# Block-decay attention and an MLP on one core: fewer unread matmuls, an earlier AV, one copy on another engine, one split step

## The chip, the cores and the metric

The kernel runs on one core of a Trainium2 chip. A core has TensorE (PE, matmuls; its weight loads are listed as PEld), VectorE (DVE), ScalarE (ACT), GpSimd (POOL) and SyncE (SP, which only issues DMAs here). Each engine works through its own instructions in program order, and engines wait for each other by semaphores. The metric is the time of one execution on the device in microseconds; lower is better.

## The reference, cut to what matters

An attention with a decay per head, computed over blocks, feeds a layer norm, a two-matrix MLP and a residual. Inputs are float32.

```python
# q, k, v: (4, 8, 768, 64); lam: one decay per head; block = 64
for b in range(nb):
    intra = einsum('bhic,bhjc->bhij', qb, kb) * Dmask      # lam^(i-j) for i >= j
    intra = einsum('bhij,bhjd->bhid', intra, vb)
    inter = einsum('bhid,bhde->bhie', qb * lam_pow, kv_state)
    out[b] = intra + inter
    kv_state = lam**64 * kv_state + einsum('bhsd,bhse->bhde', kb * rev_pow, vb)
x  = heads joined: (4, 768, 512)
xn = (x - mean) / sqrt(var + 1e-6) * g_ln
y  = x + relu(xn @ w_ch1) @ w_ch2                          # 512 -> 2048 -> 512
```

## The kernel before, in words

**Tiling.** The 768 rows of each of the 4 batches are cut into 3 windows of 256 rows. That makes 12 units of work `u` (the change's "pairs": pairs of 128-row tiles `ab` = 0, 1); units 0 to 3 are the first windows of the four batches. The MLP works on groups `g` of two tiles, one group per unit, so that group 0 is the first and group 2 the third.

**The attention of a unit.** `open_window` makes its bf16 buffers; `in_k_one`, `in_q_one`, `in_v` scale and cast the loaded k, q and v into them. `transpose_pe(u, a, pairs, eng)` (L253, L254) transposes k (`a` = 0) or q (`a` = 1) by matmuls against an identity into a PSUM tile `tp`, and one copy brings it to `kqT`: on VectorE if `eng` is given, else on ScalarE. `scores` (L282) multiplies k^T with q^T into PSUM tiles `sc` (`sce` when early), `mask` (L292, VectorE) brings them masked to `mA`. `kv` (L316) forms the products of k and v, `new_state` turns them into the running state. `av` (L428) multiplies the masked scores with v into `po`, and `inter` (L441) adds the product of q with the state, in two parts, `inter(u, 0)` and `inter(u, 1)`; between them `reader` (L452) has VectorE read a column of `po`. `norm` (L474, L475, L479 for the first two units) takes mean and variance on VectorE and writes the centred and scaled `xc`; `to_xT(u, ab)` transposes it by four matmuls (L502) and a ScalarE copy (L503) into `xT`.

**The MLP of a group.** The first matrix W1 lies in four pieces `w1[0..3]` of 512 columns, the second, W2, in four pieces as well, each loaded by one DMA that POOL issues (L117, L120). A step `m1(u)` (L539) is 8 matmuls of 256 columns over both tiles of the group, and one ReLU on ScalarE (L542) of 128x512; two steps use one piece of W1. `m1s(f, c, lo, hi)` issues the steps on piece `c`: `m1s(m1a, 2, 0, 1)` is the first of the two, `m1s(m1a, 2, 1, 2)` the second. `m1.tile(c, i)` (L650, ReLU L653) does the piece `c` for tile `i` alone: 16 matmuls of 128 columns. `m2` (L676) multiplies with W2, four matmuls of 512 columns per step; from group 4 on another form (L574) with fewer multiplications takes its place, which uses sums formed ahead on VectorE. PSUM tiles of both share the tag `mm` with four buffers, in rotation, together with `tp`, `xt` and `sce`.

**What sets the order.** The kernel is written with a manual schedule: the order of calls is the order on each engine. The head (the first 37 us) is written out by hand: units 0 and 1 with the MLP of groups 0 (`m1a`) and 1 (`m1b`) between them. After that a list `plan` holds the MLP's steps, and `units(n)` takes the next n of them between the attention steps of later units. The plan's first 20 steps are groups 0 and 1; then come the steps of group 2. Unit 2 begins with `transpose_pe(2, 0, ...)` for k^T, one step, and `transpose_pe(2, 1, ...)` for q^T.

**The start.** While the first k and q are being loaded, TensorE runs small matmuls of the identity into a tile `unread` (L180), which nothing reads, and then a matmul that spreads g_ln over the partitions (`g_all`, L183).

Of the kernel before, what the change touches and what calls it, by code (L numbers as in the profile page):

```python
# [17 lines left out]
def kernel(  # L18
# [11 lines left out]
    nc = tc.nc  # L30
# [31 lines left out]
    def mm_tile(shape, dtype, name):  # L62
        return ps.tile(shape, dtype, tag="mm", bufs=4, name=name)
# [111 lines left out]
    nc.vector.memset(ones, 1.0)  # L175
    nc.vector.tensor_copy(keep64[half[1]], keep64_b[half[1]])
    unread = ps.tile([128, 32], F32, tag="po0", name="unread")
    for _ in range(26):
        for b in range(2):
            nc.tensor.matmul(unread[half[b]], lhsT=ident[half[0], half[b]], rhs=ident[half[0], 0:32],  # L180
                             start=True, stop=True, skip_group_check=True)
# [19 lines left out]
    def open_window(u):  # L201
        kq = wk.tile([128, 2, NP, 2, 2, D], BF16, tag="kq", bufs=3, name="kq")
        vb = wk.tile([128, H, 2, D], BF16, tag="vb", bufs=4, name="vb")
        st[u] = dict(kq=kq, vb=vb)
        if u < XB:
            st[u]["kqT"] = wk.tile([128, 2, NP, 2, 128], BF16, tag="kqT", bufs=3, name="kqT")
# [40 lines left out]
    def transpose_pe(u, a, pairs, eng=None):  # L247
        s = st[u]
        n = len(pairs)
        tp = mm_tile([128, n, 2, 128], BF16, "tp")  # L250
        for i, p in enumerate(pairs):
            for j in range(2):
                nc.tensor.transpose(tp[:, i, j, :], s["kq"][:, a, p, j], ident)  # L253
        (eng.tensor_copy if eng else nc.scalar.copy)(s["kqT"][:, a, pairs[0]:pairs[0] + n], tp)  # L254
# [69 lines left out]
    def state_sum(u, ab):  # L324
        tmp = wk.tile([128, NP, D], F32, tag="Stmp", name="Stmp")
        nc.vector.tensor_tensor(tmp, st[u]["pk"][ab], state[u % B], op=ALU.add)  # L326
        return tmp
# [91 lines left out]
    def av(u, pairs, chunks=(0, 1)):  # L419
        s = st[u]  # L420
        if "po" not in s:
            s["po"] = [ps.tile([128, H, D], F32, tag=f"po{ab}", name=f"po{ab}") for ab in range(2)]
        for p in pairs:
            for e in range(2):
                for j in range(2):
                    for jq in range(2):
                        for ab in chunks:
                            nc.tensor.matmul(s["po"][ab][half[jq], 2 * p + e, :],  # L428
                                             lhsT=s[f"mA{p // 2}"][half[ab], e, p % 2, j, half[jq]],
                                             rhs=s["vb"][half[ab], 2 * p + e, j],  # L430
                                             start=(p == 0 and e == 0 and j == 0), stop=False, skip_group_check=True)

    def inter(u, first, fence=True):


        s = st[u]
        qT = s["kqT"][:, 1]
        todo = [(e, p, ab, jq) for p in range(NP) for jq in range(2)
                for e, ab in ((first, 0), (1 - first, 1)) if s["S"][ab][jq] is not None]
        for i, (e, p, ab, jq) in enumerate(todo):  # L440
            nc.tensor.matmul(s["po"][ab][half[jq], 2 * p + e, :], lhsT=qT[half[e], p, jq, half[ab]],  # L441
                             rhs=s["S"][ab][jq][half[e], p, :],
                             start=False, stop=(first == 1 and i >= len(todo) - 4), skip_group_check=True)
        if first == 0 and fence:
            reader(u)
# [8 lines left out]
    def norm(u, ab, early=False):  # L454
        s = st[u]
        po = s["po"][ab].rearrange("p h d -> p (h d)")
        if "x" not in s:
            s["x"] = xp.tile([128, 2, DM], F32, tag="x", bufs=6, name="x")
            s["mv"] = xp.tile([128, 2, 2], F32, tag="mv", name="mv")
            s["xc"] = wk.tile([128, 2, DM], BF16, tag="xc", name="xc")  # L460
        x, mv, xc = s["x"][:, ab], s["mv"][:, ab], s["xc"][:, ab]
        if u >= 2:
            if ab == 0:
                s["sum"] = xp.tile([128, 2], F32, tag="sum", name="sum")
                s["nmean"] = xp.tile([128, 2], F32, tag="nmean", name="nmean")
            sm, nm = s["sum"][:, ab:ab + 1], s["nmean"][:, ab:ab + 1]
            nc.scalar.activation(x, po, ACT.Copy, accum_out=sm)  # L467
            nc.scalar.activation(nm, sm, ACT.Copy, scale=-1.0 / DM)  # L468
            nc.vector.scalar_tensor_tensor(xc, in0=po, scalar=nm, in1=g_row, op0=ALU.add, op1=ALU.mult)  # L469
            return  # L470
        if not early:
            nc.scalar.copy(x, po)
        stats = wk.tile([128, 6], F32, tag="stats", name="stats")
        nc.vector.bn_stats(stats, po if early else x)  # L474
        nc.vector.bn_aggr(mv, stats)  # L475
        n_h = 2 if u == 0 else 1
        for h in range(n_h):
            sl = slice(h * DM // n_h, (h + 1) * DM // n_h)
            nc.vector.scalar_tensor_tensor(xc[:, sl], in0=po[:, sl], scalar=mv[:, 0:1], in1=g_row[:, sl],  # L479
                                           op0=ALU.subtract, op1=ALU.mult)  # L480
# [5 lines left out]
    def to_xT(u, ab):  # L486
        s = st[u]
        t = 2 * u + ab
        g = group_of[t]
        i = t - groups[g][0]  # L490
        if i == 0:
            xT_of[g] = gp.tile([128, KA, GT * 128], BF16, tag="xT", bufs=3, name="xT")
        dst = xT_of[g][:, :, i * 128:(i + 1) * 128]
        if u >= 2 and u not in X_PE:
            nc.sync.dma_start_transpose(dst, s["xc"][:, ab])
        else:
            if u < 2:
                xt = mm_tile([128, KA, 128], BF16, "xt")
            else:
                xt = ps.tile([128, KA, 128], BF16, tag=f"po{ab}", name="xt")  # L500
            for kk in range(KA):
                nc.tensor.transpose(xt[:, kk, :], s["xc"][:, ab, kk * 128:(kk + 1) * 128], ident)  # L502
            nc.scalar.copy(dst, xt)  # L503
# [280 lines left out]
    m1a, m2a = mlp(0)  # L784
    m1b, m2b = mlp(1)

    def m1s(f, c, lo=0, hi=2):
        n = f.count // NWC
        for u in range(c * n + lo * n // 2, c * n + hi * n // 2):
            f(u)  # L790
# [208 lines left out]
    kv(1, "sc")  # L999
    new_state(1, 0, nc.scalar)  # L1000
    m1s(m1a, 1, 1, 2)
    m1s(m1a, 2, 0, 1)
    av(1, (0, 1))
    av(1, (2, 3))
    inter(1, 0)
    norm(1, 0, early=True)
    m1s(m1a, 2, 1, 2)
    inter(1, 1)
    norm(1, 1, early=True)
    st[1]["tmp"] = state_sum(1, 1)  # L1010
    m1s(m1a, 3, 0, 1)
    to_xT(1, 0)
    m1s(m1a, 3, 1, 2)
    m1b.tile(0, 0)
    to_xT(1, 1)
    m1b.tile(1, 0)
    open_window(2)
    in_k_one(2, nc.vector, 0)
# [16 lines left out]
    plan = [(m1b.tile, c, i) for c in (2, 3) for i in range(2)]  # L1035
    plan += [(m2, i, part) for part in range(KB // 4) for m2, i in ((m2a, 0), (m2a, 1), (m2b, 0))]
    plan += [(m2b, 1, part) for part in range(KB // 4)]
    for g in range(2, len(groups)):
        m1, m2 = mlp(g)
        plan += [(m1, n) for n in range(m1.count)]  # L1040
        if g >= WG:
            plan += [(m2.w, n) for n in range(8)]
        else:
            plan += [(m2, i, part) for i in range(len(groups[g])) for part in range(KB // 4)]
# [3 lines left out]
    def units(n):  # L1048
        for _ in range(n):
            f, *a = next(steps)  # L1050
            f(*a)


    transpose_pe(2, 0, (0, 1, 2, 3))
    units(1)
    transpose_pe(2, 1, (0, 1, 2, 3))
    new_state(0, 1, nc.gpsimd)
# [314 lines left out]
```

## Time and profile before

| what | value |
|---|---|
| time, median of 3 runs | 208.91 us (208.74 to 209.30) |
| time of the profiled execution | 208.85 us |
| its span, first to last instruction | 207.1 us |
| busy in the span: PE, PEld | 198.3, 159.4 us |
| busy in the span: DVE, ACT, POOL | 133.6, 121.5, 84.7 us |
| TensorE instructions: matmuls, weight loads | 3199, 3199 |
| HBM read, written | 27.27, 6.29 MB |

The profile is that of one execution. A line of the timeline has the start, the duration, the engine, the line of the kernel, the operation with output<-inputs, the form, and in brackets the idle time of the engine before it with what ended it. In the row of slices each digit is the busy share of a fortieth of the span in tenths. In the chain of waits each row has a start, a duration and the work that the end of the kernel hung on at that time; "issue" is time without a wait that the profile shows. TensorE's matmuls overlap, so the spacing of their starts tells more than their durations.

### The profile page before, as it was taken

Reading aid. Unit: us, or ns where it says so; the run is one execution under the profiler, and the core shown is the slowest. Engines: PE = TensorE matmul, PEld = TensorE weight load, DVE = VectorE, ACT = ScalarE, POOL = GpSimd, SP = SyncE. Lnnn points to the kernel's source line nnn. Section 1 sums busy time; section 2 is a strip of 40 time slices with the busy share of each in tenths; the row PEclk is TensorE's granted clock in tenths of the full one; section 3 lists DMA queues with packets and bytes.
Section 4 is the critical chain, followed back from the end, with each engine's and each line's share of the span. In section 5 each row is a group of like instructions: output and inputs, shape, how many; then the busy total and the mean of one; then the engine's idle time right before and its main releaser. Section 6 shows DMA issues by size and latency. Waiting matters only on the chain.

```text
span 207.1 us, 7435 instructions
## 1 busy us (share of the span) xinstructions
PE 198.3 (96%) x3199; PEld 159.4 (77%) x3199; DVE 133.6 (65%) x276; ACT 121.5 (59%) x279; POOL 84.7 (41%) x117
## 2 busy tenths in 40 slices
PE   4989999999999999999999999999999999999992
PEld 3468889544685687488888888888888888988881
DVE  3686480526964459867898775776876947865253
ACT  3775668726258358257565775585596565652620
POOL 5658059027747260266264440782282202002020
PEclk9999999999999999999999999999999999999999
DMA  4999999999899999999999999897958020158403
GB/s 105 302 256 216 165 293 188 213 279 258 231 211 278 218 168 171 183 256 171 196 202 128 188 202 170 205 213 163 190 109 181 3 51 3 24 117 278 143 14 92
DMA packets 91011, 36.41 MB, mean 176 GB/s; under 512 B 65121, under 2 KB 88161, under 8 KB 90978
## 3 DMA queue, kind: packets, MB, share of 16 engines
q1 hardware_dynamic: 86368, 31.53, 73.5%
q0 software_dynamic: 4224, 4.19, 12.5%
q8 instruction: 25, 0.41, 0.8%
q10 hardware_dynamic: 386, 0.20, 0.4%
q14 instruction: 8, 0.07, 0.1%
HBM read 27.27 MB, written 6.29 MB: 162 GB/s over the span
## 4 chain that ended last, share of the span: by engine, by line
PE 86%; ACT 6%; DVE 2%; DMA 2%; issue 1%; POOLq 0%; POOL 0%; DVEq 0%
PE pm L539 37%; PE pm L676 14%; PE pwd L574 6%; PE pwa L574 6%; PE pwc L574 6%; PE pm1t L650 3%; PE pwb L574 3%; PE po L441 2%; DMA lam_b<-in_lam_dram 2%; PE tp L253 2%; PE po L428 2%; ACT kqT L254 1%; DVE x L587 1%; PE po L415 1%; PE xt L502 1%
## 5 line engine op out<-in xcount | busy, mean ns | idle before, releaser
L539 PE MATMUL pm<-xT,w 128*128 128x256 bf16 x688 | 78.5, 273 | 0.0
L539 PEld LDWEIGHTS <-w 128*128 128x128 bf16 x688 | 66.0, 98 | 8.8 <-DVE Smid L397 0.3
L542 ACT ACTIVATE hT<-pm 128x512 f16<-128x512 f32 x86 | 50.4, 596 | 30.9 <-PE pm L539 30.8
L676 PE MATMUL pm<-w,hT 128*128 128x512 f16 x128 | 29.8, 380 | 0.0
L574 PEld LDWEIGHTS <-hs 128*128 128x128 f16 x256 | 24.9, 98 | 2.9
L599 POOL TENSOR_TENSOR x<-ev_u,x 128x256 f32<-128x256 f32 x8 | 5.8, 724 | 51.8 <-ACT ev_u L598 40.4
L322 POOL TENSOR_TENSOR Sn<-Stmp,lam_s 128x256 bf16<-128x256 f32 x16 | 9.8, 616 | 36.8 <-DVE Stmp L326 15.7
L557 DVE TENSOR_TENSOR hs<-hT 128x1024 f16<-128x1024 f16 x16 | 13.8, 864 | 16.5 <-ACT hT L542 16.5
L676 PEld LDWEIGHTS <-hT 128*128 128x128 f16 x128 | 11.7, 98 | 12.5
L574 PEld LDWEIGHTS <-hT 128*128 128x128 f16 x192 | 18.8, 98 | 2.2
L469 DVE SCALAR_TENSOR_TENSOR xc<-po,nmean,g_row 128x512 bf16<-128x512 f32 x18 | 13.0, 745 | 5.1 <-ACT nmean L468 5.0
L467 ACT ACTIVATE x<-po 128x512 f32<-128x512 f32 x18 | 10.6, 591 | 7.7 <-PE po L441 4.5
L292 DVE TENSOR_TENSOR mA<-sc,keep 128x512 bf16<-128x512 f32 x14 | 9.0, 684 | 8.8 <-PE sc L282 8.8
L512 ACT ACTIVATE sq<-x,nmean 128x512 bf16<-128x512 f32 x18 | 12.9, 719 | 0.3
L245 POOL TENSOR_TENSOR vb<-vin,lam_v 128x1024 bf16<-128x1024 f32 (+1 forms) x7 | 11.6, 1658 | 3.4 <-DMA vin<-in_v_dram 3.2
L245 POOL TENSOR_TENSOR vb<-vin,lam_p 128x1024 bf16<-128x1024 f32 x6 | 11.6, 1928 | 0.8 <-DMA vin<-in_v_dram 0.8
L650 PE MATMUL pm1t<-xT,w 128*128 128x128 bf16 x160 | 11.2, 229 | 0.1
L650 PEld LDWEIGHTS <-w 128*128 128x128 bf16 x160 | 10.1, 103 | 0.7 <-issue 0.6
L587 DVE SCALAR_TENSOR_TENSOR x<-pwd,rstd,x 128x256 f32<-128x256 f32 x16 | 7.7, 482 | 3.6 <-POOL x L607 3.6
L239 POOL TENSOR_TENSOR kq<-qin,lam_p 128x512 bf16<-128x512 f32 x9 | 9.3, 1042 | 1.6 <-DMA qin<-in_q_dram 1.6
L587 DVE SCALAR_TENSOR_TENSOR x<-pwa,rstd,x 128x512 f32<-128x512 f32 (+1 forms) x16 | 9.1, 612 | 0.8
L574 PE MATMUL pwa<-w,hT 128*128 128x256 f16 x64 | 9.6, 273 | 0.0
(134 smaller groups left out, 315.5 us busy)
## 6 DMA issues: line engine op xcount, KB each, us to landing
out_dram<-x SPq DMA_DIRECT2D x22, 256.0 KB, 4.0
w<-in_moe_w_ch_dram POOLq DMA_DIRECT2D x8, 512.0 KB, 8.6
kin<-in_k_dram SPq DMA_DIRECT2D x14, 256.0 KB, 5.5
qin<-in_q_dram SPq DMA_DIRECT2D x14, 256.0 KB, 4.9
vin<-in_v_dram SPq DMA_DIRECT2D x14, 256.0 KB, 4.8
kin<-in_k_dram SPq DMA_DIRECT2D x5, 512.0 KB, 6.3
qin<-in_q_dram SPq DMA_DIRECT2D x5, 512.0 KB, 7.6
vin<-in_v_dram SPq DMA_DIRECT2D x5, 512.0 KB, 6.5
```

The costliest lines, as they stand in the source:

```text
L245: eng.tensor_tensor(st[u]["vb"][:, hs], qkv_in[u]["v"][:, hs], lv.to_broadcast([128, n, 2, D]), op=ALU.mult)
L322: eng.tensor_tensor(dst, src, lam_s[:, :, None].to_broadcast([128, NP, D]), op=ALU.mult)
L467: nc.scalar.activation(x, po, ACT.Copy, accum_out=sm)
L469: nc.vector.scalar_tensor_tensor(xc, in0=po, scalar=nm, in1=g_row, op0=ALU.add, op1=ALU.mult)
L512: nc.scalar.activation(sq, s["x"][:, ab], ACT.Square, bias=s["nmean"][:, ab:ab + 1], accum_out=ss[:, ab:ab + 1])
L539: nc.tensor.matmul(pm[:, b, :], lhsT=w1[n // W2K][:, kk, (n % W2K) * 128:(n % W2K + 1) * 128], rhs=xT_of[g][:, kk, 0:N], start=(b == 0 and ...
L542: nc.scalar.activation(hT[:, u * NB:(u + 1) * NB, 0:N], pm, ACT.Relu)
L557: nc.vector.tensor_tensor(s13, b[:, :, 1:2, :].to_broadcast([128, n, 2, 128]), b[:, :, 0:4:3, :], op=ALU.subtract)
L574: nc.tensor.matmul(pr[bank], lhsT=lhs(r), rhs=rhs, start=(first and r == 0), stop=(r == KB // 2 - 1), skip_group_check=True)
L587: nc.vector.scalar_tensor_tensor(out, in0=in0, scalar=r[ab], in1=in1, op0=ALU.mult, op1=ALU.add)
L650: nc.tensor.matmul(pm[:, b, :], lhsT=w1[c][:, kk, b * 128:(b + 1) * 128], rhs=xT_of[g][:, kk, i * 128:(i + 1) * 128], start=(b == 0 and kk ...
L676: nc.tensor.matmul(acc[i], lhsT=hT[:, kk, i * 128:(i + 1) * 128], rhs=w2[kk // W2K][:, kk % W2K, :], start=(kk == 0), stop=(kk == KB - 1))
```

## The change

Four edits. The unread matmuls go from 52 to 36, which with their weight loads are 32 instructions. In the hand-written head, the second unit's `av`, `inter` and `norm` go ahead of the first step on W1's third piece, and the steps of pieces 3 and 4, the transposes of the second unit's `xc` and the tiles of group 1 are interleaved anew. The third unit's k^T is copied out of PSUM by VectorE instead of ScalarE. And the first two steps of the third group, 8 matmuls over both tiles each, become two `m1.tile` steps of 16 matmuls over one tile each, on the same piece of W1.

```diff
     unread = ps.tile([128, 32], F32, tag="po0", name="unread")
-    for _ in range(26):
+    for _ in range(18):
         for b in range(2):
             nc.tensor.matmul(unread[half[b]], lhsT=ident[half[0], half[b]], rhs=ident[half[0], 0:32],
                              start=True, stop=True, skip_group_check=True)
...
     kv(1, "sc")
     new_state(1, 0, nc.scalar)
     m1s(m1a, 1, 1, 2)
-    m1s(m1a, 2, 0, 1)
     av(1, (0, 1))
     av(1, (2, 3))
     inter(1, 0)
     norm(1, 0, early=True)
-    m1s(m1a, 2, 1, 2)
+    m1s(m1a, 2, 0, 1)
     inter(1, 1)
     norm(1, 1, early=True)
     st[1]["tmp"] = state_sum(1, 1)
+    m1s(m1a, 2, 1, 2)
+    to_xT(1, 0)
     m1s(m1a, 3, 0, 1)
-    to_xT(1, 0)
-    m1s(m1a, 3, 1, 2)
     m1b.tile(0, 0)
     to_xT(1, 1)
+    m1s(m1a, 3, 1, 2)
     m1b.tile(1, 0)
...
-        plan += [(m1, n) for n in range(m1.count)]
+        plan += [(m1.tile, 0, 0), (m1.tile, 0, 1)] if g == 2 else [(m1, 0), (m1, 1)]
+        plan += [(m1, n) for n in range(2, m1.count)]
...
-    transpose_pe(2, 0, (0, 1, 2, 3))
+    transpose_pe(2, 0, (0, 1, 2, 3), nc.vector)
     units(1)
     transpose_pe(2, 1, (0, 1, 2, 3))
```

## The prediction, made before the result was known

> **What bounds the kernel now.** I read the page first: busy shares, then the row of slices.
>
> ```profile
> PE 198.3 (96%) x3199; PEld 159.4 (77%) x3199; DVE 133.6 (65%) x276; ACT 121.5 (59%) x279; POOL 84.7 (41%) x117
> ...
> PE   4989999999999999999999999999999999999992
> ```
>
> TensorE has work from the second slice to the last. Busy is not peak, so I took the spacing of matmul starts in the trace: after 37 us it is the ordinary one almost everywhere (216 ns at 512 columns, 109 to 111 ns at 256, 56 ns at 128). A change of order there gains nothing; only holes in TensorE's stream do. I looked for them in the chain of waits (start us, us, what), between 26 and 38 us:
>
> ```profile
> 27.60 0.60 ACT hT L542
> 28.20 0.48 ACT xT L503
> 28.68 0.04 issue
> 28.72 1.07 PE pm1t L650 x16
> 29.79 0.02 issue
> 29.82 0.60 ACT hT L653
> 30.41 0.48 ACT xT L503
> 30.90 0.04 issue
> 30.94 1.96 PE pm1t L650 x32
> ...
> 33.52 0.97 ACT x L484 x2
> 34.48 0.92 ACT kqT L254
> 35.40 0.50 ACT hT L653
> 35.90 0.91 ACT kqT L254
> 36.82 0.04 issue
> 36.86 0.42 PE sc L282 x16
> ```
>
> Three times TensorE stands behind ScalarE. In starts: the matmul at 28.72 comes 337 ns after the one before, where 110 is ordinary (0.23 us lost); that at 30.94 after 262 instead of 56 (0.21 lost); the scores at 36.86 after 573. Ordinary there is 149: a change from a full to a small tile costs 93 ns beside the matmul itself (202 ns start to start after 256 columns, 309 after 512), and 56 + 93 = 149; so 0.42 us is lost. The third is two k/q copies, 1.06 us each, behind two copies of x.
>
> Then TensorE's timeline ahead of the first W1 tile:
>
> ```profile
> 15.05 0.31 PE L441 MATMUL po<-Sn,kqT 64*64 64x64 bf16 x4
> 16.04 0.32 PE L441 MATMUL po<-Sn,kqT 64*64 64x64 bf16 x4 [0.67 <-issue]
> 16.29 0.61 PE L253 MATMUL tp<-ident,kq 128*128 128x128 bf16 x4
> 16.69 1.91 PE L650 MATMUL pm1t<-xT,w 128*128 128x128 bf16 x16
> ```
>
> Eight matmuls of one loop are cut in two, with no semaphore between the halves: start to start 0.91 us. Last, the list of waits of TensorE for the head:
>
> ```profile
> PE g_all L183 <- DVE keep L176: 1.2, 1, 1.2
> ```
>
> The matmul behind the unread ones waits 1.2 us for VectorE anyway.
>
> **What the Trainium skill says.** "Runtime: NRT & Kernel Launch", Instruction fetch mechanics: engines refill instructions in blocks of 16 KiB, 256 instructions, and a crossing is mostly hidden. The page has 25 instruction packets of together 0.41 MB on queue 8, so 16 KB each, and 6398 TensorE instructions: it fits. The first of them starts at 13.66 us, and the cut above follows it, at about the 449th TensorE instruction; so here a crossing is seen. At later packets no hole appears. "TensorE: Matmul & The Clock Gate", Part 1: The HAM clock gate: cold TensorE runs at half speed until a busy window of a free-running 3.41 us has passed. The trace agrees: 128-column matmuls start every 107 ns until 19.1 us and every 56 ns from 20.4 us; its clock record begins full speed at 20.5 us. "VectorE: DVE Perf Modes", Why PSUM operands drop a tier: a 16-bit copy out of PSUM can still go at twice the rate. The four kqT copies by VectorE take 418 ns for 128x512, against ScalarE's 586: it agrees.
>
> **The change, part by part.**
>
> *Sixteen unread matmuls with their weight loads go.* Fifty-two start between 1.43 and 2.79 us, 27 ns apart: 16 x 27 = 0.43 us of TensorE time, worth nothing, since g_all starts at 4.18 behind VectorE's copy (ends 4.07). If that cover went, 0.43 us. But every later instruction stands 32 places earlier, so the fetch boundary falls 32 named instructions later: behind the other four matmuls of the state product and four transposes, at about the eighth matmul of the first W1 tile. TensorE reached this at 17.4 us; the block was there at 16.04. The fetch will start a little later, since the sequencer has 32 more instructions to issue; I expect it still in time, and no hole. What is late next: the first W1 piece. Its DMA issued at 8.07 took 8.5 us, landing at 16.58, and the tile started at 16.69. So of 0.88 us pause, 0.05 us is gained; bounds: 0 to 0.11 us. VectorE's normalisation (statistics at 16.39, idle 1.01 us before) comes up to 0.9 us earlier, but TensorE gets to its transposes only at 18.82, paced by itself: nothing.
>
> *AV of the second pair ahead of W1's third piece.* No instruction is added. TensorE's order becomes: half of piece 2, AV, half of piece 3, second state product, half of piece 3, transposes, half of piece 4, tile (0,0) of group 1, transposes, the last half of piece 4, tile (1,0). AV starts at 24.52 - 0.87 = 23.65; its masks are done at 22.56 and the state from ScalarE at 23.82, while the state product comes only at 24.18. VectorE's reader, statistics and centring follow 0.87 earlier: xc(1,0) at 26.30, transposes at 26.53 (before: 27.17 and 27.40). The stretch up to tile (0,0) is the old one shifted by one step of 0.87 us, so its 0.23 us hole stays: still activation, xT copy, tile on ScalarE. The step that was displaced now stands behind the second transposes: ScalarE gets 0.88 us more for the second xT, so the hole at 30.94 closes: -0.21 us. W1 pieces: third landed at 23.49, needed now at 24.42 (before 23.54, on its heels); fourth landed at 26.05, needed at 26.75 and 28.96. The moved steps issue no DMA and nothing on POOL, so SP's and POOL's queues keep their order. VectorE's later casts move from 29.03 to about 28.15; k has landed by 27.89, q's wait at 30.14 remains, and its user is TensorE at 34 us.
>
> *k^T of the third pair copied by VectorE.* ScalarE loses 1.06 us between 34.36 and 35.40; VectorE gains one 128x1024 copy, not shown there: between 0.42 x 2 = 0.84 and, at ScalarE's rate, 1.06 us; I take 0.84. VectorE is idle for 6.49 us before its masks at 37.31; behind the copy only those wait. It runs from about 33.2 to 34.0. ScalarE, worked forward: x until 34.3, one activation until 34.8, q^T until 35.75. TensorE, 0.21 us ahead, has finished its two tiles at about 36.1, so the scores no longer wait: -0.42 us. If ScalarE is late after all, I get back between 0 and 0.42.
>
> *Two tiles in the third group.* Two steps of 8 matmuls at 109 ns (0.874 us each; 54.33 to 57.82 for four) become two of 16 at 56 ns (0.891 us each, from 28.72 to 29.61): +0.035 us, bounds 0 to 0.1. ScalarE evicts 512 columns each in either form; its inputs were ready at 51.2, the steps begin at 54.3. These add 32 instructions, so from there fetch boundaries stand as before.
>
> Sum: -0.05 - 0.21 - 0.42 + 0.04 = **-0.64 us**. TensorE takes that to the end: W2's last piece landed at 45.93 and is needed after 48; kqT of pairs 3 and 4 landed at 54.16 and 63.47, used at 58.2 and 70.3. Against the profiled execution's own 208.85 us (span 207.1 and 1.75 around it) this gives 208.21; the median shown is 0.06 higher, which is scatter. I say **208.2**.
>
> **Rivals.**
> 1. *The fetch hole moves into the first W1 tile.* It decides if the block lands after about 17.4 us. For it: in the old trace the queue ran dry with only some 30 instructions in hand at the packet's start. Against: without the cut TensorE stands some 0.6 us ahead of W1's landing, time in which the block can come. Price: up to 0.88 us on the path, and by thinning the window before 20.5 us it may put full speed off by one window, half of 3.41 = 1.71 us. 208.2 + 0.88 = 209.1; with the clock, 210.8.
> 2. *The gain is eaten.* q^T at 35.75 against scores at 36.1 has 0.35 us in hand; if VectorE's copy stands behind a POOL operation at 33.28 (1.92 us), or the clock phase slips, the holes close only in part: 208.6 to 208.9.
> 3. *The clock comes one window earlier*, since the pause before the dense tiles is gone. For it: work up to 20.4 is at half speed. The second W1 piece lands at 20.65 and was used at 21.33: at most 0.68 us more, 207.5.
> 4. *It does not do what it says* (the boundary is elsewhere): the first term is 0, the rest stays: 208.3.
>
> **How the numbers follow.** My forecast with case 4 has 0.61, rival 1 0.11, rival 2 0.16, rival 3 0.12. A measurement here tells about 0.3% from no change, so below 208.28 is faster and above 209.54 slower. The forecast stands close to the edge: 0.46 of its 0.61 faster, 0.15 same; rival 3 faster; rival 2 0.13 same and 0.03 slower by some new wait; rival 1 slower. Faster 0.58, same 0.28, slower 0.14. Range 207.4 (rival 3, with the best ends) to 209.2 (rival 1 without the clock).
>
> **What would show it.** Right: no cut in the state product near 15 us; first W1 tile at 16.6 to 16.7; AV at 23.65; a hole of 0.2 us ahead of tile (0,0) but none ahead of (0,1); VectorE's kqT copy of 0.7 to 0.9 us near 33; scores of the third pair within 0.15 us of the tile before. Wrong: a pause inside the first W1 tile, full clock later than 20.5 us, or scores still released by ScalarE's copy.

## The result, and the profile after

In 22 executions of each kernel the changed one has a median of 209.18 us (208.23 to 211.07) and the one before 209.34 us (208.31 to 211.51). The ratio is **0.9995, 95% interval 0.997 to 1.0019**: no difference that this comparison can tell, where 208.2 us and a gain of 0.3% were forecast. The level was missed too: the three executions shown ahead of the prediction (208.74 to 209.30, median 208.91) all lie below the median of the 22, whose spread is 3.2 us.

The profiled execution of the changed kernel took 210.09 us, with a span of 208.3 us, 1.2 us more than the one of before. First the same rows of the page:

```profile
PE 198.5 (95%) x3199; PEld 159.1 (76%) x3199; DVE 135.6 (65%) x277; ACT 120.7 (58%) x278; POOL 84.9 (41%) x117
...
PE   3989999999999999999999999999999999999991
```

VectorE has one instruction more and ScalarE one fewer; TensorE has as many as before. Next, TensorE's timeline ahead of the first W1 tile:

```profile
15.62 0.42 PE L441 MATMUL po<-Sn,kqT 64*64 64x64 bf16 x8
15.99 0.29 PE L253 MATMUL tp<-ident,kq 128*128 128x128 bf16 x1
16.57 0.50 PE L253 MATMUL tp<-ident,kq 128*128 128x128 bf16 x3 [0.29 <-POOL kq L229]
16.87 1.92 PE L650 MATMUL pm1t<-xT,w 128*128 128x128 bf16 x16
```

The state product is whole now (x8 in one row), and the tile still starts just behind the landing of W1's first piece, 16.81 us in this execution. Then the two stretches where ScalarE held TensorE up, from the same timeline, and VectorE's copies of kqT (count, duration in ns min/median/max):

```profile
28.40 1.05 PE L650 MATMUL pm1t<-xT,w 128*128 128x128 bf16 x16
29.29 0.39 PE L502 MATMUL xt<-ident,xc 128*128 128x128 bf16 x4
29.51 1.04 PE L539 MATMUL pm<-xT,w 128*128 128x256 bf16 x8
30.39 1.28 PE L650 MATMUL pm1t<-xT,w 128*128 128x128 bf16 x20
...
34.85 1.95 PE L650 MATMUL pm1t<-xT,w 128*128 128x128 bf16 x32
36.73 0.42 PE L282 MATMUL sc<-kqT 64*64 64x128 bf16 x16
```

```profile
L254 DVE COPY kqT<-tp x5: 414/419/690, 9.2 to 33.7; 128x512 bf16<-128x512 bf16 x4, 128x1024 bf16<-128x1024 bf16 x1
```

The hole of 0.21 us ahead of tile (0,1) is gone; the one of 0.42 us ahead of the third pair's scores is gone (149 ns from the last tile matmul, the ordinary step), with a VectorE copy of 0.69 us. So the two gains that made up the forecast are in the profile. What took its place? The chain of waits of this execution near 48 us, and TensorE's timeline there:

```profile
33.85 14.79 DMA w<-in_moe_w_ch_dram
48.63 0.04 issue
48.67 1.02 PE pm L676 x4
```

```profile
47.92 0.39 PE L502 MATMUL xt<-ident,xc 128*128 128x128 bf16 x4
48.67 1.02 PE L676 MATMUL pm<-w,hT 128*128 128x512 f16 x4 [0.37 <-DMA w<-in_moe_w_ch_dram]
```

W2's last piece landed at 48.63, 2.7 us later than in the profile of before, and TensorE waited. In starts of matmuls, the measure of the holes above, 0.53 us are lost there and 0.18 at W2's third piece (landing 44.94): together 0.71 us, more than the whole forecast. Already the first small DMA, the decays, issued at 0.81 us in both, landed 0.46 us later (5.02 against 4.56), and W1's first load was issued 0.46 us later (8.53 against 8.07): part of the lateness was there before the change could act.

### The profile page after: what moved, and what is told of

Its sections match the earlier page's. It is cut to its first block, busy times and chain, and to the rows that moved or that the text cites. A ratio compares the mean times of both kernels' runs of the same rounds, so it can differ in the third digit from the quotient of the medians.

```text
span 208.3 us, 7435 instructions
## 1 busy us (share of the span) xinstructions
PE 198.5 (95%) x3199; PEld 159.1 (76%) x3199; DVE 135.6 (65%) x277; ACT 120.7 (58%) x278; POOL 84.9 (41%) x117
## 4 chain that ended last, share of the span: by engine, by line
PE 72%; DMA 18%; SPq 3%; POOL 2%; DVE 2%; issue 1%; POOLq 0%; ACT 0%; DVEq 0%
PE pm L539 33%; DMA w<-in_moe_w_ch_dram 11%; PE pm L676 10%; DMA qin<-in_q_dram 7%; PE pwd L574 6%; PE pwc L574 6%; PE pwa L574 6%; PE pwb L574 3%; SPq L76 3%; PE po L441 1%; DVE x L587 1%; PE po L415 1%; PE po L428 1%; PE sc L362 1%; PE pm1t L650 1%; PE pk L381 1%
## 5 line engine op out<-in xcount | busy, mean ns | idle before, releaser
L539 PE MATMUL pm<-xT,w 128*128 128x256 bf16 x672 | 76.9, 273 | 0.1
L542 ACT ACTIVATE hT<-pm 128x512 f16<-128x512 f32 x84 | 49.2, 596 | 25.5 <-PE pm L539 25.3
L557 DVE TENSOR_TENSOR hs<-hT 128x1024 f16<-128x1024 f16 x16 | 14.4, 898 | 16.3 <-ACT hT L542 16.3
L650 PE MATMUL pm1t<-xT,w 128*128 128x128 bf16 x192 | 13.0, 228 | 0.1
L653 ACT ACTIVATE hT<-pm1t 128x512 f16<-128x512 f32 x12 | 7.3, 605 | 9.0 <-PE pm1t L650 8.9
```

The costliest lines, as they stand in the source:

```text
L539: nc.tensor.matmul(pm[:, b, :], lhsT=w1[n // W2K][:, kk, (n % W2K) * 128:(n % W2K + 1) * 128], rhs=xT_of[g][:, kk, 0:N], start=(b == 0 and ...
L542: nc.scalar.activation(hT[:, u * NB:(u + 1) * NB, 0:N], pm, ACT.Relu)
L557: nc.vector.tensor_tensor(s13, b[:, :, 1:2, :].to_broadcast([128, n, 2, 128]), b[:, :, 0:4:3, :], op=ALU.subtract)
L650: nc.tensor.matmul(pm[:, b, :], lhsT=w1[c][:, kk, b * 128:(b + 1) * 128], rhs=xT_of[g][:, kk, i * 128:(i + 1) * 128], start=(b == 0 and kk ...
```

## The experiments

Three theories stood at first. **A**: W2's landing, which hangs on a chain of DMAs and POOL work without TensorE, eats the gain. **B** (later D): the change gains nothing, its new order costs as much elsewhere. **C**: the gain is there and hidden in the scatter. All ratios below are against executions of the kernel before on the same chip (67 for the runs e, 59 for h, 43 for i); each variant has 14 or 22.

### No wait for W2's later pieces: e1 and e2

```diff
-                nc.tensor.matmul(acc[i], lhsT=hT[:, kk, i * 128:(i + 1) * 128], rhs=w2[kk // W2K][:, kk % W2K, :],
+                nc.tensor.matmul(acc[i], lhsT=hT[:, kk, i * 128:(i + 1) * 128], rhs=w2[0 if g < 2 else kk // W2K][:, kk % W2K, :],
```

> The kernel before, with the W2 steps of groups 0 to 3's first two (groups 0 and 1) reading W2's first piece for all four parts; this leaves out the other three pieces there, and so takes away TensorE's wait for their landing. Theory A (the landing of W2's last pieces, a chain of DMAs and POOL work that has no TensorE in it, decides when TensorE passes 49 us in many executions): 0 to 0.4% faster than before, since in the slower executions TensorE waits for them in the kernel before too. Theory B (the new order costs as much elsewhere as it gains): within 0.1% of before. Theory C (the gain of 0.6 us is there and hidden in the scatter): within 0.1% of before.

> The changed kernel with the same W2 steps reading the first piece alone (the same part left out). Theory A: the 0.6 us that the closed holes give now reach the end, so 0.3 to 0.6% faster than before and about 0.3% (0.6 us) faster than the kernel before with the same edit. Theory B: no faster than the kernel before with the same edit. Theory C: 0.3% faster than before, as the changed kernel itself.

Measured: e1, the edit on the kernel before, 0.9973 (0.9956 to 0.9991); e2, on the changed kernel, 0.9995 (0.9968 to 1.0022). Theory A wanted e2 ahead of e1; it is not, though A's number for e1 came true. C missed both (1 and 0.997 were expected), and B missed e1. In the profiles of e1 and of h3, h4 and i4 (below; each with a part of the change) TensorE needs 17.24 to 17.26 us from the third pair's scores to the start of the last W2 matmul, as in the kernel before, so these executions had no such wait to remove. Others may have had one, as the changed kernel's first profile has. Why e1 is faster than before, and e2 is not, stays open.

The trace of e1 shows a wait of the old order that the first profile had only just missed, in TensorE's timeline:

```profile
22.04 1.05 PE L539 MATMUL pm<-xT,w 128*128 128x256 bf16 x8
23.27 0.94 PE L539 MATMUL pm<-xT,w 128*128 128x256 bf16 x7 [0.18 <-DMA w<-in_moe_w_ch_dram]
```

TensorE's full clock began at 18.9 us there (20.5 in the profile of before), it came early to W1's third piece, and lost 0.34 us beyond the ordinary step. With AV ahead of that step, this wait is in none of the profiles of the new order. A wait for W1's second piece is in two of them: 0.27 us in the changed kernel's first profile (landing 21.82), 0.73 in i2 (21.61).

### W2 loaded earlier: e3, and the change again: e4

```diff
-    behind(qkv_in[2]["k"][:, 0, 0, 0:1])
+    behind(w1[3][:, 0, 0:1])
     load_w2(0)
     load_w2(1)
```

> The changed kernel, with the four W2 loads behind the landing of W1's last piece instead of behind the landing of the third pair's k: POOL issues them some 2 us earlier. Theory A: W2's last piece lands 1 to 2 us earlier, TensorE no longer waits for it, 0.2 to 0.5% faster than before, unless the third pair's q comes so much later that TensorE waits for it near 34 us. Theories B and C: no change against the changed kernel (within 0.1%).

> The changed kernel again, unedited, for a second profile and a second comparison. Theory A: ratio to before 0.998 to 1.001, with a wait for W2's third or last piece where it lands after 44 or 48 us. Theory B: ratio 1.000. Theory C: ratio 0.997. In every theory the holes ahead of the tile (0,1) and ahead of the third pair's scores stay closed.

Measured: e3 0.9975 (0.9955 to 0.9995), e4 0.9968 (0.995 to 0.9987). W2's last piece landed at 44.51 us in e3 and at 45.53 in e4, needed at 46.84 and 47.00. The edit moved less than was expected: W2's first two pieces were issued at 26.38 and 27.18 us (28.78 and 29.58 in e4), but the last two, whose loads stand further down in the kernel, at 32.00 and 32.80 (31.58 and 32.38 in e4). So e3 tests A only in part. It is no faster than e4, and e4, the change itself, is faster than before this time: for C. The chain of waits in e4 now runs over TensorE from the one hole that was forecast to stay:

```profile
26.34 0.60 ACT hT L542
26.94 0.48 ACT xT L503
27.43 0.04 issue
27.47 1.05 PE pm1t L650 x16
28.52 0.22 PE xt L502 x4
28.74 0.87 PE pm L539 x8
29.62 2.68 PE pm1t L650 x48
32.30 0.45 PE tp L253 x8
32.74 0.89 PE pm1t L650 x16
33.64 0.45 PE tp L253 x8
34.08 1.79 PE pm1t L650 x32
35.87 0.35 PE sc L282 x16
```

### The change a third and a fourth time: h1 and i3

> The changed kernel once more, unedited, for the size of its effect: the first comparison gave a ratio of 0.9995 (0.997 to 1.0019), the second 0.9968 (0.995 to 0.9987). Theory C (the closed holes are worth what the prediction said, 0.64 us or 0.3%, and the scatter between executions hid it in the first comparison): ratio 0.9955 to 0.9985. Theory D (the changed kernel is as fast as the one before; the second comparison was the lucky one): ratio 0.9985 to 1.0015. In the profile the state product near 15 us is whole, and the holes ahead of tile (0,1) and of the third pair's scores are closed.

> The changed kernel, unedited, beside the others on this chip. Theory C (the closed holes are worth 0.64 us): ratio 0.9955 to 0.9985; theory D (no effect): 0.9985 to 1.0015.

Measured: h1 0.9972 (0.9955 to 0.9988), i3 0.9982 (0.9959 to 1.0005). With the first comparison and e4 that makes four: 0.9995, 0.9968, 0.9972, 0.9982. Weighted by their intervals the mean is 0.9977, and 0.9967 to 0.9986 if they are taken as independent; each has its own executions of the kernel before (22, 67, 59 and 43). So the change gains about 0.23%, 0.5 us, and theory C holds in the main; e2, the change beside e1, does not fit it.

### The parts alone: h3, h4 and i4

```diff
 h3 (before with the copy only)
-    transpose_pe(2, 0, (0, 1, 2, 3))
+    transpose_pe(2, 0, (0, 1, 2, 3), nc.vector)
 h4 (before with the order only): the second part of the change's diff
 i4 (before with the counts only)
-    for _ in range(26):
+    for _ in range(18):
...
-        plan += [(m1, n) for n in range(m1.count)]
+        plan += [(m1.tile, 0, 0), (m1.tile, 0, 1)] if g == 2 else [(m1, 0), (m1, 1)]
+        plan += [(m1, n) for n in range(2, m1.count)]
```

> The kernel before with the third pair's k^T copied by VectorE, and nothing else of the change. Theory C: the hole ahead of the third pair's scores (0.42 us in the profile) closes, the other two stay; ratio to before about 0.998. Theory D: the hole closes and comes back as another wait behind it; ratio 1.000.

> The kernel before with the new order of the second pair's steps, and nothing else of the change. Theory C: the hole ahead of tile (0,1), 0.21 us, closes, and the wait for W1's third piece (0.34 us in the profile of e1_before_one_piece, none in that of before) can't arise; the scores of the third pair still wait for ScalarE's copy, by up to 0.42 us or more, since TensorE comes to them earlier while ScalarE's row of work is as long; so ratio 0.998 to 1.000. Theory D: ratio 1.000.

> The kernel before with 16 unread matmuls fewer and the first two steps of group 2 as tiles, and neither the new order nor the other copy. Every theory: the state product near 15 us is whole, and nothing is gained by it, as W1's first piece lands at 16.6 us; 0.04 us for the tiles; ratio 0.999 to 1.001. If it is below 0.999, the fetch near 15 us cost time in the kernel before.

Measured: h3 0.9999 (0.9981 to 1.0017), h4 0.9985 (0.9967 to 1.0002), i4 0.9997 (0.9979 to 1.0016). None can be told from 1 alone. The 0.998 that C expected of h3 lies just outside h3's interval; D's number, 1.000, came true. The sum of the three, -0.19%, is near the whole's -0.23%, but its error is about 0.3%. Their traces are plainer. In h3 the scores follow the tiles without a hole (150 ns from start to start); in h4 the hole ahead of tile (0,1) is gone while the scores still wait. One line from h3, two from h4:

```profile
36.38 0.42 PE L282 MATMUL sc<-kqT 64*64 64x128 bf16 x16
```

```profile
30.23 2.84 PE L650 MATMUL pm1t<-xT,w 128*128 128x128 bf16 x48
37.05 0.42 PE L282 MATMUL sc<-kqT 64*64 64x128 bf16 x16 [0.35 <-ACT kqT L254]
```

That wait is 0.42 us beyond the ordinary step, as in the kernel before: it neither grew, as the expectation allowed, nor shrank. So each of the two edits closes a hole of its own. In i4 the state product is whole, and its end is seen to be worthless, since TensorE then waits for W1:

```profile
15.20 0.42 PE L441 MATMUL po<-Sn,kqT 64*64 64x64 bf16 x8
15.55 0.61 PE L253 MATMUL tp<-ident,kq 128*128 128x128 bf16 x4
16.48 1.89 PE L650 MATMUL pm1t<-xT,w 128*128 128x128 bf16 x16 [0.32 <-DMA w<-in_moe_w_ch_dram]
```

### Where the other pauses come from: h2, i1 and i2

In most profiles a later AV is cut, in either order. TensorE's timeline of h3 shows the longest case:

```profile
61.85 0.44 PE L428 MATMUL po<-vb,mA 64*64 64x64 bf16 x31
63.36 0.47 PE L428 MATMUL po<-vb,mA 64*64 64x64 bf16 x33 [1.07 <-issue]
```

The cut is at TensorE's 1985th instruction. The one near 15 us in the kernel before is at the 449th: 6 x 256 earlier. Three experiments moved these boundaries.

```diff
 h2 (the changed kernel, six tiles in group 2)
-        plan += [(m1.tile, 0, 0), (m1.tile, 0, 1)] if g == 2 else [(m1, 0), (m1, 1)]
-        plan += [(m1, n) for n in range(2, m1.count)]
+        plan += [(m1.tile, c, i) for c in range(3) for i in range(2)] if g == 2 else [(m1, n) for n in range(6)]
+        plan += [(m1, n) for n in range(6, m1.count)]
 i1 (the changed kernel, tiles in the head; c = 1 and 2); i2 is i1 with the W2 loads of e3
-    m1s(m1a, c, 0, 1)
+    m1a.tile(c, 0)
...
-    m1s(m1a, c, 1, 2)
+    m1a.tile(c, 1)
```

> The changed kernel, with the first six instead of the first two steps of group 2 as tiles: 64 more TensorE instructions and 0.07 us more work ahead of the AV of the fourth pair. In the profiles of four kernels that AV is cut in two by 0.16 to 0.92 us at TensorE's 1985th instruction, 6 x 256 after the 449th where the state product near 15 us was cut. Theory E (both are instruction fetches, on the path in the second place): the boundary comes to lie just ahead of this AV, among matmuls of 256 columns, the AV is whole in the profile, and the time is 0.1 to 0.4 us (0.05 to 0.2%) below the changed kernel's. Theory F (the AV waits for data that VectorE or a DMA brings late): the AV is cut at the same matmul as before, and the time is 0.07 us above the changed kernel's.

> The changed kernel, with the four steps of group 0 on W1's second and third piece as tiles: 64 more TensorE instructions in the head and 0.07 us more work. So the fetch boundaries at the 1473rd and the 1985th instruction, which lie inside the AVs of the third and the fourth pair and cut them by 0 to 0.25 and by 0 to 1.26 us in the profiles so far, come to lie at the start of these AVs or ahead of them. Theory E (instruction fetches are on the path there): both AVs whole or cut by under 0.1 us; 0.1 to 0.4 us below the changed kernel. Theory F (the AVs wait for data): cut as before; 0.07 us above the changed kernel.

> The same, with the four W2 loads behind the landing of W1's last piece, as in e3_after_w2_early. Theory A (W2's last piece binds often): 0.1 to 0.4 us below i1_after_head_tiles. Otherwise: the same as i1_after_head_tiles within 0.2 us. Against before, if both E and A hold: ratio 0.994 to 0.997.

Measured: h2 0.9995 (0.9972 to 1.0019), i1 1.0017 (0.9996 to 1.0039), i2 0.9995 (0.9977 to 1.0013). Theory E's prediction for the place came true, against theory F, by which the AV waits for data: the fourth pair's AV is whole in all three. Of i1:

```profile
61.47 0.71 PE L428 MATMUL po<-vb,mA 64*64 64x64 bf16 x64
62.01 0.30 PE L441 MATMUL po<-Sn,kqT 64*64 64x64 bf16 x8
```

Its prediction for the time did not. Other waits came instead: in h2 the third tile stands 0.55 us at 55.98, because VectorE, busy with W2's sums, is late to free a PSUM tile; in i1 0.46 us go at W2's last piece (47.1), and 0.15 ahead of the second pair's AV (22.88), where the profile names ScalarE's state (L341), which ended just then; and in i2 the pause is at the 3265th, 449 + 11 x 256, by the chain of waits:

```profile
91.95 1.31 PE pm L539 x12
93.26 0.49 issue
93.75 1.27 PE pm L539 x10
```

i2 is 0.3 us below i1 (209.20 against 209.52), as theory A expected of the earlier loads, but their intervals overlap. No variant beats the changed kernel. Nor did one of these runs time the pauses by themselves.

## Why the prediction was wrong, and where it was right

**"TensorE takes that to the end", against one execution's own 208.85: this step failed.** It took the rest of the profiled execution as fixed. From the third pair's scores (36.86 us in the profile of before) to the end of the span that execution took 170.24 us, the least of all 14 profiles; the others took 170.3 to 172.0, the changed kernel's first 171.6. So in that first profile TensorE is 0.13 us earlier at the scores and 1.2 later at the end: 0.71 us go at W2's landings, 0.32 at the 1985th instruction, and another 0.3 lie behind the start of the last matmul.

The forecast of 208.2 is 0.98 us below the measured median. Half of that is the level: the kernel before has a median of 209.34 in 22 executions, 0.49 above the 208.85 taken, and "the median shown is 0.06 higher, which is scatter" had judged the scatter from three executions within 0.56 us. The other half is the gain: 0.16 us between the medians instead of 0.64, and about 0.5 in the four comparisons together. A comparison of 22 against 22 tells a difference from about 0.25% on, half its interval: the 0.31% forecast lies just beyond that, the 0.23% found does not. So the first comparison could easily miss the gain; the chance of 0.28 for "same" was too low for that reason. Of 80 executions of the changed kernel 7 took 208.25 us or less, of 191 of the kernel before 2.

**The two holes: right, in place and nearly in size.** Forecast -0.63 us. The stretch from the start of tile (0,0) to the third pair's scores lies behind the start of the full clock in every profile, and so is free of its scatter. It takes 8.14 us with the old order and copy (before, e1, i4), 7.66 with the copy alone (h3), 8.81 with the order alone (h4) and 8.33 in all six profiles that keep the changed head (after, e2, e3, e4, h1, i3). The new order has one W1 step of 0.88 us more in it, so the order is worth 8.14 + 0.88 - 8.81 = 0.21 us and the copy 0.48 with either order, 0.05 more than its hole, since one step inside the tiles ahead of the scores is shorter too: together -0.69. The hole of 0.23 us ahead of tile (0,0) stayed in all six, as forecast. VectorE's copy took 0.69 us where 0.84 was taken: doubling the 0.42 doubled its fixed part as well (419 ns for 512 columns, 690 for 1024). That VectorE's copies are faster than ScalarE's, 418 against 586 ns, does not by itself show the twofold rate that the prediction reads from it.

**The unread matmuls: right.** Forecast 0.05 us; i4 shows TensorE waiting for W1's first piece instead. **The tiles: right.** Forecast +0.035 us; from the end of the W2 steps to the fourth pair's AV the traces of four kernels with the old steps take 8.22 to 8.23 us and five of the six changed ones 8.27 or 8.28: +0.045. The sixth, i3, lost another 0.17 us at 57.28.

**The margins on the way to the end: half wrong.** The 2 us at W2's last piece came from one execution. In the four profiles of the changed kernel itself W2's last piece landed at 48.63 (late, see above), 45.53, 46.41 and 47.54 us; in the other three TensorE did not wait, with 1.5 us in hand in e4 and 0.7 in i3. Whether the change makes W2 later is not settled: its first load was issued at 28.3 to 29.1 us in the five profiles with the old order or parts of the change, and at 28.8 to 30.6 in these four and e2. And "at later packets no hole appears" was nearly true of the profile of before (0.13 us at the 2497th instruction), and of that only: at the 1985th instruction the pauses are 0, 0.91, 1.25, 0 and 0.15 us in five profiles of kernels with the old order or its parts, and 0.31, 0.82, 0.18, 0, 0.20 and 0.42 in six of the changed order. They are no cost of the change, but the longest exceed its gain, so the profile of one execution of each kernel orders them by chance.

**The rivals.** The hole did not move into the first W1 tile: in every profile with 36 unread matmuls the 449th instruction, in that tile, follows its packet (the DMA that brings the next 256 instructions) by 2.9 to 3.5 us and is not late. The clock did not visibly move with the change: full speed begins between 17.8 and 22.2 us in the 14 profiles, and in the kernels with 52 unread matmuls alone between 18.9 and 21.3. So the changed kernel's first profile shows a sign that the prediction lists under wrong, full clock later than 20.5 us (20.9), without its meaning anything. What stays of the second rival, the eaten gain, is the difference between 0.64 forecast and about 0.5 measured, which the intervals do not separate. One step of the chances does not follow: the first rival without the clock, 209.1 us, is booked as slower, though by the prediction's own limits (208.28 and 209.54) it is the same. Open are e1's 0.27%, e2 beside it, and why h3's closed hole does not show in its time.

## What to carry to other kernels

Before forecasting a third of a per cent, ask how far executions of the same kernel spread, and take a margin at a DMA's landing from several profiles, not from one. Holes that the traces show closed in every execution are better evidence for a small gain than the end-to-end times of a few. A count of instructions on the engine that sets the time is a parameter of its own: it decides which matmuls the fetch boundaries fall on; the three placings tried here moved the pause, and none was faster.

## What the runs showed of the hardware that was not expected

- The pauses without a semaphore lie at TensorE's instructions 449, 705 (in h2), 1473, 1985, 2497 and 3265, counted over matmuls, weight loads and waits, all 449 + 256 n, in different executions. That agrees with the Trainium skill, "Runtime: NRT & Kernel Launch", Instruction fetch mechanics, on blocks of 256 instructions; its "mostly hidden" holds for most of the 24 boundaries of a profile, and the longest pause was 1.25 us.
- At the pauses of 0.6 us and more whose packet was read, the next instruction comes 2.2 to 2.7 us after the start of the instruction packet: 13.66 and 16.04, 60.74 and 63.36, 73.41 and 76.11, 91.20 and 93.75 us. A boundary that TensorE reaches sooner after the packet is late by the rest. The 1985th instruction was reached 1.36 to 3.38 us after the packet in the eleven profiles in which it lies inside the AV.
- The beginning of the full clock differs by 4.4 us between the 14 profiles, and by 2.9 us (19.3 to 22.2) between four executions of the changed kernel. The Trainium skill, "TensorE: Matmul & The Clock Gate", Part 1: The HAM clock gate, calls the window free-running and run-variable; these runs agree: full speed lasts 187.73 us in ten profiles and 184.32 in four, 3.41 apart.
